# Gated linear attention and a gated MLP in one kernel: outputs issued in two steps, fewer dummy matmuls, a fused state update

## The chip, the cores and the metric

The kernel runs on one core of a Trainium2 chip. The engines that matter here are PE (matrix multiply, with weight loads as instructions of their own, PEld in the profile), DVE (elementwise vector work and scans), ACT (elementwise work with a lookup function), and SP, which here only issues transfers. PE writes to PSUM banks, DVE and ACT read them. The metric is the device time of one execution in microseconds, lower is better, as the median of several runs.

## What is computed

A recurrence over 768 tokens for 4 batches of 8 heads gives y; y, reordered to 3072 tokens of 256 features, goes through a gated MLP. The reference, cut to what matters:

```python
for c in range(nc):                      # chunks of 32 tokens
    cum = np.cumsum(log_a[chunk])
    M = (C @ B.T) * exp(cum_i - cum_j) * causal
    y = M @ x + (C @ state) * exp(cum)
    state = exp(sum(log_a)) * state + sum_j(B_j x_j * exp(cum_last - cum_j))
g = y @ w_gate                           # 3072 x 256 by 256 x 1536
out = (silu(g) * (y @ w_val)) @ w_out    # back to 256
```

x is 4 x 8 x 768 x 32, B and C have 16 states, all in float32.

## The kernel before

The tokens are cut into NB = 6 blocks of 128 (for each of the 4 batches), and the recurrence inside a block into K = 2 pieces of 64. For block k the attention part has these steps, by the names that tiles carry in the profile:

- L and E: running products of the decays, made by scans on DVE (`scan_j`, `scan_n`); for block 0 a part of the decays is spread over the partitions by PE first (`a`, `spread`). xb holds x and B, bc holds B and C; DVE weighs the B in xb by L (`weigh_b`) and the C in bc by E (`weigh_c`). Cz is C with the two heads of a pair apart.
- st: sums of B and x over a piece, on PE (`sums`); `apart` copies them into T, the state's tile, DVE one part and ACT the other.
- S: the scores C B on PE (`scores`); `mix` multiplies them into L, four DVE operations, called M in the plan.
- `step`: the state from one piece to the next, T = T + decay x older T.
- y: `outputs` puts, batch by batch, `values` (16 matmuls of L and xb) and `carried` (8 of bc and T) into four PSUM banks. In float32 each of these matmuls stands in the trace as two records, so a block's y are 192. For block 0 they are issued apart: first all `values` in two groups, then `carried`.

The MLP part then multiplies y with the weights:

- For block 0, y is copied as it is (xf), and used with the rounded float32 weights. For later blocks it is split into a high part xh and a low part xl in a shorter format, and each product is made of three matmuls (high x high, high x low, low x high).
- gv: gate and value matmuls, for NF = 12 groups f of 128 hidden columns, named gv k, f, and 0 or 1. In block 0 one matmul is two records. `silu` on ACT and `product` on DVE make sg. sg is split into hh (`hid_high`, ACT or DVE) and hl (`hid_low`, DVE).
- po: the output matmuls (`project`), `drain` copies them to ob, `store` sends them out.
- The weights arrive as 64-bit numbers. For each piece w DVE and ACT round them to float32 in about seven operations (`w_magnitude` to `w_round`); `w_high` (wh) and `w_low` (wl) split the result for blocks 1 to 5.

No instruction order is written out by hand. Every step is an entry of `plan.add`: engine, estimated cost, rank (a due time), what it needs, which buffers it takes and frees. `Plan.order` simulates the engines with these costs and issues on each engine, of the steps that could begin first, the one with the lowest rank; the list that comes out is each engine's program order, fixed when the program is built. `clocked` is its model of PE's speed: half speed until a window of 3.4133 us had been active enough (AWAKE). One engine name, "-", stands for steps without an instruction.

Dummies: `idle` issues three matmuls of a constant tile, unit, with itself (rest in the profile; nothing reads their result). The table IDLE gives their ranks in two lists: 23 entries (69 matmuls) before block 0's scores are mixed and 24 (72 matmuls) after.

Buffers: L, E, bc, xb and Cz exist once, so loads for a block wait for the outputs of the one before. T exists twice, tmp twice, PSUM banks are four for mm (gv, po, and S and y of block 0) and four for at (st, S and y, and the dummies). sg has SG = 21 places, and rounded weights w of the twelve gate groups take twelve of these until they are split.

Of the kernel before, what the change touches and what calls it, by code (L numbers as in the profile page):

```python
# [9 lines left out]
F32 = mybir.dt.float32  # L10
# [5 lines left out]
ALU = mybir.AluOpType  # L16
# [3 lines left out]
P = 128  # L20


Q = 64
K = P // Q
T = BATCH * P
# [17 lines left out]
class Plan:  # L43
# [5 lines left out]
    BIAS = 0.0  # L49
    WINDOW, AWAKE = 3.4133, 1.28  # L50
    SWITCH = {"Act": 1.28, "PE": 0.09}
# [51 lines left out]
    def clocked(self, t, cost, rows):  # L103

        while cost > 1e-9:
            w = int(t / self.WINDOW + 1e-9)
            rate = 1.0 if self.active.get(w - 1, 0.0) >= self.AWAKE else 0.5
            d = min(cost / rate, (w + 1) * self.WINDOW - t)
            self.active[w] = self.active.get(w, 0.0) + d * rate * rows
            cost -= d * rate  # L110
            t += d
        return t
# [90 lines left out]
def scan_moe_kernel(ctx: ExitStack, tc, aj, an, bc, xb, wgv, wo, cst, sel, out):  # L203
# [238 lines left out]
    def step(k, q):  # L442

        E = bl[k]["E"]
        t = att.tile([P, BATCH, 2 * D], F32, tag="tmp", name=f"tmp{k}_{q}", bufs=2)
        new = bl[k]["T"][:, q]
        decay = E[:, :, q, Q:].to_broadcast([P, BATCH, 2 * D])
        ve.tensor_tensor(out=t, in0=state(k, q), in1=decay, op=ALU.mult)
        ve.tensor_tensor(out=new, in0=new, in1=t, op=ALU.add)

# [31 lines left out]

    def outputs(k):
        for b in range(BATCH):
            values(k, (b,), (0, 1))
            carried(k, b)
# [179 lines left out]
    def do(f, *a):  # L666
        return lambda *e: f(*a, *e)


    plan = Plan(  # L670
        dict(mm=4, at=4, L=1, E=1, bc=1, xb=1, Cz=1, T=2, tmp=2, raw=4, w=1, x=2, hh=HB, sg=SG, ob=2),
        dict(SP=5.2, Act=3.0, DVE=1.0, PE=1.5, Pool=2.0, **{"-": 0.7}),
    )
# [30 lines left out]
    for i in range(NW):  # L704
# [8 lines left out]
        if i < NF:  # L713
            r = due(1, i) - LATER
        add([("Act", 0.6), ("DVE", 0.36)], None, do(w_high, i), r - 2.7, [("round", i)], gives=("wh", i))
        whole_done = [("gv", 0, i, m) for m in range(2)] if i < NF else []
# [8 lines left out]
    for k in range(NB):  # L725
# [20 lines left out]
        if not k:  # L746
# [4 lines left out]
            for b in range(BATCH):  # L751
# [6 lines left out]
                if b >= SPREAD:  # L758
                    add("DVE", 0.35, do(clip_j, b), r - 0.5, ["aj"], gives=("clip", b))
                    add("DVE", 1.14, do(scan_j, 0, b), r, [("clip", b), "dj"], gives=("L", 0, b))  # L760
            add("DVE", 0.35, clip_n, -1.4, ["an"], gives="clip_n")
            add("DVE", 1.17, do(scan_n, 0), -1.3, ["clip_n"], gives=("E", 0))
        else:
# [24 lines left out]
        for q in range(0 if k else 1, len(st)):  # L788
            need = [*before, ("E", k), ("ap", k, q)] + ([] if k or q > 1 else [("ap", k, 0)])
            add("DVE", 0.75, do(step, k, q), z + (8 if k else 25) + q, need, takes=[("tmp", ("tmp", k, q))], uses=[("tmp", k, q)] + ([("T", k - 1)] if k and not q else []), gives=("step", k, q))  # L790
            before = [("step", k, q)]
# [7 lines left out]
        if k:  # L799
            need = [*(("M", k, p) for p in range(NP)), ("ce", k), *steps]  # L800
            add("PE", 3.2, do(outputs, k), z + 11, need, takes=[("at", i) for i in y], uses=[L, *uses], gives=("y", k), kind="f", slack=SLACK)
        for b in range(0 if k else BATCH):
# [13 lines left out]
    for k in range(NB):  # L816
        xs = [(t, k, i) for t in ("xh", "xl") for i in range(2 * K)]
        for f in range(NF):
# [13 lines left out]
            h = ("h", k, f)  # L832
            add([("Act", 0.6), ("DVE", 0.36)], None, do(hid_high, k, f), r, [("pr", k, f)], takes=[("hh", h)], uses=[t], gives=("hh", k, f))
            add("DVE", 0.6, do(hid_low, k, f), r + 1, [("hh", k, f)], uses=[t, h], gives=("hl", k, f))
# [20 lines left out]
SPREAD = 3  # L855
IDLE = [-9.0] * 8 + [-3.8, -3.3, -2.8] + [-1.2 + 0.1 * i for i in range(12)], [15.0 + 0.5 * i for i in range(24)]
LATER = 3.0
# [55 lines left out]
```

## Time and profile before

| | us |
|---|---|
| median of 3 runs | 369.84 |
| lowest and highest run | 366.42, 373.3 |
| the profiled execution | 368.33 |
| its span, first to last instruction | 366.6 |
| PE busy | 357.5 (98%) |
| DVE busy | 231.0 (63%) |
| ACT busy | 127.0 (35%) |

The profile's busy time of PE contains dummies, and matmuls at half clock; it says when PE had something in it, not how much was done. The view of waits lists, for each engine and tile, what ended the idle time before it; "issue" means that nothing the profile shows did. The chain of waits is followed back from the last instruction and shown in order of time, neighbours merged. Every instruction carries line 192, the helper that records the order, so that work is told apart by tiles, not by lines.

### The profile page before, as it was taken

To read this page: it belongs to the slowest core of one execution; us is meant where nothing else is said; L and a number is where in the kernel's file an instruction comes from. 1 tells how busy PE (TensorE), PEld (TensorE's weight loads), DVE (VectorE), ACT (ScalarE), POOL (GpSimd) and SP (SyncE) were. 2 spreads that over 40 slices of the span, in tenths; PEclk is the share of its full clock that TensorE was granted. 3 is DMA by queue.
4 is the path that set the end of the run, shared out by engine and by line. 5 is a ranking of instruction groups with operands and counts; after the bars stand their busy time and mean duration, and the time that the engine had idled before them with its cause. 6 is when DMAs were issued, how large, how long until landed. Compare 5 with 4: busy or idle time off the path is not lost.

```text
span 366.6 us, 7587 instructions
## 1 busy us (share of the span) xinstructions
PE 357.5 (98%) x3293; PEld 276.0 (75%) x3293; DVE 231.0 (63%) x409; ACT 127.0 (35%) x225; POOL 0.8 (0%) x6
## 2 busy tenths in 40 slices
PE   8989999999999999999999999899999899999996
PEld 6855445488877888877788877688878688888895
DVE  3899999989999693663367554359345334352241
ACT  3275684444234543121342221323312133221242
POOL 0000000000000000000000000000000000000000
PEclk9999999999999999999999999899999999999999
DMA  6749742880101921000550000570100000100001
GB/s 181 283 134 285 240 146 87 237 224 2 58 2 46 207 95 59 0 3 2 172 119 25 35 2 2 143 148 2 57 0 3 4 0 2 57 0 2 0 0 59
DMA packets 8737, 28.62 MB, mean 78 GB/s; under 512 B 1008, under 2 KB 1912, under 8 KB 8064
## 3 DMA queue, kind: packets, MB, share of 16 engines
q1 hardware_dynamic: 8704, 28.14, 26.3%
q8 instruction: 26, 0.43, 0.5%
q14 instruction: 7, 0.06, 0.0%
HBM read 24.79 MB, written 3.35 MB: 77 GB/s over the span
## 4 chain that ended last, share of the span: by engine, by line
PE 94%; DVE 3%; issue 2%; ACT 0%; ACTq 0%
PE gv L192 55%; PE po L192 27%; PE y L192 5%; PE rest L192 3%; PE S L192 2%; PE a L192 1%; PE st L192 1%; DVE L L192 1%; DVE wo4w L192 0%; DVE sg L192 0%; DVE wo3w L192 0%; DVE wo4l L192 0%; DVE wo3l L192 0%; ACT wo5w L192 0%; ACT wo4w L192 0%
## 5 line engine op out<-in xcount | busy, mean ns | idle before, releaser
L192 DVE TENSOR_TENSOR sg<-gv,sg 128x512 f32<-128x512 f32 x72 | 49.4, 687 | 83.0 <-PE gv L192 80.6
L192 ACT ACTIVATE sg<-gv 128x512 f32<-128x512 f32 x72 | 42.9, 596 | 108.8 <-PE gv L192 108.6
L192 DVE TENSOR_TENSOR hl<-sg,hh 128x512 fp32r<-128x512 f32 x72 | 48.6, 685 | 17.5 <-ACT hh L192 17.0
L192 ACT CAST hh<-sg 128x512 fp32r<-128x512 f32 x56 | 34.9, 622 | 46.1 <-PE po L192 35.6
L192 DVE TENSOR_TENSOR_SCAN L<-L,dj 128x520 f32<-128x520 f32 x21 | 25.8, 1233 | 1.0 <-DMA L<-clipped 1.0
L192 DVE TENSOR_TENSOR L<-S,L 128x512 f32<-128x512 f32 x24 | 15.4, 682 | 2.2 <-PE S L192 2.2
L192 PEld LDWEIGHTS <-unit 128*128 128x128 bf16 x141 | 11.5, 122 | 4.9 <-issue 3.7
L192 PE MATMUL y<-L,xb 64*32 64x64 f32 x768 | 11.7, 223 | 3.2 <-issue 3.2
L192 ACT COPY ob<-po 128x512 f32<-128x512 f32 (+1 forms) x13 | 7.2, 555 | 21.3 <-PE po L192 20.8
L192 PE MATMUL rest<-unit 128*128 128x128 bf16 x141 | 12.9, 263 | 1.0 <-DVE warm L192 1.0
L192 PEld LDWEIGHTS y<-L,xb 64*32 64x32 f32 x768 | 7.6, 105 | 5.8 <-issue 3.9
L192 PE MATMUL y<-bc,T 32*64 32x64 f32 x352 | 10.2, 229 | 1.2 <-issue 1.2
L192 PEld LDWEIGHTS y<-bc,T 32*64 32x64 f32 x352 | 7.2, 131 | 4.5 <-issue 2.7
L192 PE MATMUL po<-hh,wo0h 128*128 128x512 f32 (+1 forms) x26 | 9.9, 382 | 0.0
L192 DVE CAST xh<-y 128x256 fp32r<-128x256 f32 x8 | 3.0, 418 | 10.9 <-PE y L192 10.9
L192 PE MATMUL po<-hh,wo2h 128*128 128x512 f32 (+1 forms) x26 | 9.8, 378 | 0.0
L192 PE MATMUL po<-hl,wo5h 128*128 128x512 f32 (+1 forms) x26 | 9.8, 377 | 0.0
L192 ACT CAST xh<-y 128x256 fp32r<-128x256 f32 x12 | 3.8, 379 | 17.1 <-PE y L192 17.1
L192 PE MATMUL po<-hl,wo0h 128*128 128x512 f32 (+1 forms) x26 | 9.7, 374 | 0.0
L192 PE MATMUL po<-hh,wo1h 128*128 128x512 f32 (+1 forms) x26 | 9.7, 373 | 0.0
L192 PE MATMUL po<-hl,wo3h 128*128 128x512 f32 (+1 forms) x26 | 9.7, 373 | 0.0
L192 PE MATMUL po<-hh,wo0l 128*128 128x512 f32 (+1 forms) x26 | 9.7, 373 | 0.0
(285 smaller groups left out, 800.5 us busy)
## 6 DMA issues: line engine op xcount, KB each, us to landing
L<-clipped SPq DMA_DIRECT2D x10, 520.0 KB
xb<-in_xb SPq DMA_DIRECT2D x6, 768.0 KB, 12.0
bc<-in_bc SPq DMA_DIRECT2D x6, 512.0 KB, 3.8
out<-ob SPq DMA_DIRECT2D x11, 256.0 KB, 2.2
E<-clipped SPq DMA_DIRECT2D x5, 260.0 KB
wg0r<-in_wgv SPq DMA_DIRECT2D x1, 512.0 KB
wg1r<-in_wgv SPq DMA_DIRECT2D x1, 512.0 KB
wg2r<-in_wgv SPq DMA_DIRECT2D x1, 512.0 KB, 9.9
```

Of the source, the lines that this page charges most:

```text
L192: ins = getattr(self.engine, name)(*a, **k)
```

## The change

- `outputs` takes the batches to do. For blocks 1 to 5 the plan has it twice, for batches 0 and 1 and for 2 and 3, with a step on an engine "~" of no instructions between them, which lets 2.6 us of planned time pass before the second half. The first half's slack against its inputs is larger.
- `step` is one fused multiply-add per batch, in place: four operations of 128 x 64 in place of two of 128 x 256. The buffer tmp goes.
- Splitting in block 0 is held back: `w_high` of the twelve gate weights and `hid_high` of block 0 need the last mix of block 1, ("M", 1, NP - 1).
- IDLE has 8 entries ahead and 14 with a rank of 1000, which are taken when PE has nothing else by the plan.
- The plan's clock is taken as slow before its time 17 (COLD). Ranks of `clip_n` and `scan_n` of block 0 are a little later, and the planned cost of `step` is 0.55 in place of 0.75.

```diff
-            rate = 1.0 if self.active.get(w - 1, 0.0) >= self.AWAKE else 0.5
+            rate = 1.0 if t >= self.COLD and self.active.get(w - 1, 0.0) >= self.AWAKE else 0.5
...
-        t = att.tile([P, BATCH, 2 * D], F32, tag="tmp", name=f"tmp{k}_{q}", bufs=2)
-        new = bl[k]["T"][:, q]
-        decay = E[:, :, q, Q:].to_broadcast([P, BATCH, 2 * D])
-        ve.tensor_tensor(out=t, in0=state(k, q), in1=decay, op=ALU.mult)
-        ve.tensor_tensor(out=new, in0=new, in1=t, op=ALU.add)
+        new, old = bl[k]["T"][:, q], state(k, q)
+        for b in range(BATCH):
+            ve.scalar_tensor_tensor(
+                new[:, b], old[:, b], E[:, b, q, Q:], new[:, b], ALU.mult, ALU.add
+            )
...
-    def outputs(k):
-        for b in range(BATCH):
+    def outputs(k, bs):
+        for b in bs:
             values(k, (b,), (0, 1))
             carried(k, b)
...
-        add([("Act", 0.6), ("DVE", 0.36)], None, do(w_high, i), r - 2.7, [("round", i)], gives=("wh", i))
+        later = [("M", 1, NP - 1)] if i < NF else []
+        add([("Act", 0.6), ("DVE", 0.36)], None, do(w_high, i), r - 2.7, [("round", i), *later], gives=("wh", i))
...
-            add("PE", 3.2, do(outputs, k), z + 11, need, takes=[("at", i) for i in y], uses=[L, *uses], gives=("y", k), kind="f", slack=SLACK)
+            add("PE", 1.6, do(outputs, k, (0, 1)), z + 11, need, takes=[("at", i) for i in y], uses=y, gives=("y", k, 0), kind="f", slack=min(k - 0.5, 2.5))
+            add("~", 2.6, lambda: None, z, [("y", k, 0)], gives=("pause", k))
+            add("PE", 1.6, do(outputs, k, (2, 3)), z + 11, [("pause", k)], uses=[L, *uses], gives=("y", k), kind="f")
...
-            add([("Act", 0.6), ("DVE", 0.36)], None, do(hid_high, k, f), r, [("pr", k, f)], takes=[("hh", h)], uses=[t], gives=("hh", k, f))
+            add([("Act", 0.6), ("DVE", 0.36)], None, do(hid_high, k, f), r, [("pr", k, f)] + ([] if k else [("M", 1, NP - 1)]), takes=[("hh", h)], uses=[t], gives=("hh", k, f))
...
-IDLE = [-9.0] * 8 + [-3.8, -3.3, -2.8] + [-1.2 + 0.1 * i for i in range(12)], [15.0 + 0.5 * i for i in range(24)]
+IDLE = [-9.0] * 8, [1000.0] * 14
```

What this does to the order is seen in the built programs. The dummies: before there are 141 of them (23 and 24 entries of three), in the change 66. Ahead of the first gv the change has the same 24 at the very start, then none until the outputs of block 0 are issued, and then 21; those that stood between the a matmuls (9), between st and y of block 0 (36) and within y (3) are gone, and st of block 0 stands whole ahead of its y, where half of it stood amid y. Between the gv of block 0 there were 45 up to the fourth group; the change has none up to the seventh, 9 behind it, and 12 ahead of S of block 1.

PE, around the outputs of block 3 (y3): before, the whole of y is followed by gv of group 9 of block 2.

```order
L192 MATMUL y3_2_1967<-bc3_1488,T3_1494 64x64
L192 MATMUL y3_3_1968<-bc3_1488,T3_1494 64x64
L192 MATMUL gv2_9_0_2066<-xh2_979,wg9h_887 128x512 x2
L192 MATMUL gv2_9_0_2066<-xh2_979,wg9l_966 128x512 x2
L192 MATMUL gv2_9_0_2066<-xl2_980,wg9h_887 128x512 x2
L192 MATMUL gv2_9_1_2086<-xh2_979,wg9h_887 128x512 x2
L192 MATMUL gv2_9_1_2086<-xh2_979,wg9l_966 128x512 x2
L192 MATMUL gv2_9_1_2086<-xl2_980,wg9h_887 128x512 x2
```

In the change the same gv stand behind batch 1, and the third batch's y follows.

```order
L192 MATMUL y3_2_1899<-bc3_1441,T3_1447 64x64
L192 MATMUL y3_3_1900<-bc3_1441,T3_1447 64x64
L192 MATMUL gv2_9_0_1950<-xh2_893,wg9h_839 128x512 x2
L192 MATMUL gv2_9_0_1950<-xh2_893,wg9l_884 128x512 x2
L192 MATMUL gv2_9_0_1950<-xl2_894,wg9h_839 128x512 x2
L192 MATMUL gv2_9_1_1957<-xh2_893,wg9h_839 128x512 x2
L192 MATMUL gv2_9_1_1957<-xh2_893,wg9l_884 128x512 x2
L192 MATMUL gv2_9_1_1957<-xl2_894,wg9h_839 128x512 x2
L192 MATMUL y3_0_1897<-L3_1445,xb3_1466 32x64
L192 MATMUL y3_2_1899<-L3_1445,xb3_1466 32x64
```

Blocks 4 and 5 are alike. In block 2 the twelve matmuls between the halves are po of block 0, in block 1 the four (eight records) of gv of block 0's group 10; y of block 1 begins behind group 9, where before it began behind group 8.

DVE, ahead of the first gv: before, this stands between the end of the mixing of block 0 and the copy of y (xf) that the first gv needs; ISA is the rounding addition.

```order
L192 TENSOR_TENSOR T0_108<-st0_1_220,cs_78 128x256
L192 TENSOR_SCALAR all_99<-all_99 128x6x64
L192 TENSOR_SCALAR wg0w_238<-wg0w_238 128x512
L192 TENSOR_SCALAR wg1w_306<-wg1w_306 128x512
L192 TENSOR_SCALAR wg0w_238<-wg0w_238 128x512
L192 TENSOR_SCALAR wg2w_375<-wg2w_375 128x512
L192 SCALAR_TENSOR_TENSOR wg0w_238<-wg0r_152,wg0w_238 128x512
L192 TENSOR_SCALAR wg2w_375<-wg2w_375 128x512
L192 ISA wg0w_238<-wg0r_152,wg0w_238 128x1024
L192 COPY xf_131<-y0_1_272 128x4x64
```

In the change (from wg1's first operation on) two more weight operations and a second copy come ahead of its end.

```order
L192 TENSOR_SCALAR wg1w_227<-wg1w_227 128x512
L192 TENSOR_SCALAR wg0w_195<-wg0w_195 128x512
L192 TENSOR_SCALAR wg2w_257<-wg2w_257 128x512
L192 SCALAR_TENSOR_TENSOR wg0w_195<-wg0r_145,wg0w_195 128x512
L192 TENSOR_SCALAR wg2w_257<-wg2w_257 128x512
L192 ISA wg0w_195<-wg0r_145,wg0w_195 128x1024
L192 SCALAR_TENSOR_TENSOR wg2w_257<-wg2r_153,wg2w_257 128x512
L192 TENSOR_SCALAR wg1w_227<-wg1w_227 128x512
L192 COPY xf_131<-y0_0_304 128x4x64
L192 COPY xf_131<-y0_1_305 128x4x64
```

Further ahead on DVE, the clip of L for the batch that is loaded directly moves from behind the third scan of block 0 to behind the first, and all four weighings of xb stand ahead of the scan of E and the mixes, where three stood between the mixes.

DVE, between the early gv of block 0: before, the splitting of groups 0 and 1 (wg0l, wg1l, hl) stands here, ahead of L of block 1.

```order
L192 TENSOR_TENSOR wg0l_513<-wg0w_238,wg0h_442 128x512
L192 ISA wg4w_470<-wg4r_429,wg4w_470 128x1024
L192 TENSOR_TENSOR sg0_1_504<-gv0_1_1_506,sg0_1_504 128x512
L192 TENSOR_TENSOR wg1l_544<-wg1w_306,wg1h_461 128x512
L192 TENSOR_TENSOR hl0_0_495<-sg0_0_456,hh0_0_494 128x512
L192 TENSOR_TENSOR hl0_1_547<-sg0_1_504,hh0_1_546 128x512
```

In the change it begins behind the last mix of block 1 (the first row), and hl of block 0 later still.

```order
L192 TENSOR_TENSOR L1_369<-S1_3_640,L1_369 128x4x2x64
L192 ISA wg10w_538<-wg10r_499,wg10w_538 128x1024
L192 TENSOR_SCALAR wg11w_594<-wg11w_594 128x512
L192 TENSOR_TENSOR wg0l_696<-wg0w_195,wg0h_689 128x512
L192 TENSOR_SCALAR wg11w_594<-wg11w_594 128x512
L192 TENSOR_TENSOR wg1l_753<-wg1w_227,wg1h_694 128x512
L192 SCALAR_TENSOR_TENSOR wg11w_594<-wg11r_540,wg11w_594 128x512
L192 TENSOR_TENSOR sg0_9_755<-gv0_9_1_684,sg0_9_755 128x512
L192 ISA wg11w_594<-wg11r_540,wg11w_594 128x1024
L192 TENSOR_TENSOR wg2l_769<-wg2w_257,wg2h_750 128x512
```

Of these twelve low halves ten stood behind the mixes before, too, from group 2 on. On SP the loads of block 2 change their order: bc goes ahead of L and E.

More of the change, by code (lines that the diff above doesn't have):

```diff
@@ L49 @@
     BIAS = 0.0
-    WINDOW, AWAKE = 3.4133, 1.28
+    WINDOW, AWAKE, COLD = 3.4133, 1.28, 17.0
     SWITCH = {"Act": 1.28, "PE": 0.09}
@@ L670, in scan_moe_kernel @@
     plan = Plan(
-        dict(mm=4, at=4, L=1, E=1, bc=1, xb=1, Cz=1, T=2, tmp=2, raw=4, w=1, x=2, hh=HB, sg=SG, ob=2),
-        dict(SP=5.2, Act=3.0, DVE=1.0, PE=1.5, Pool=2.0, **{"-": 0.7}),
+        dict(mm=4, at=4, L=1, E=1, bc=1, xb=1, Cz=1, T=2, raw=4, w=1, x=2, hh=HB, sg=SG, ob=2),
+        dict(SP=5.2, Act=3.0, DVE=1.0, PE=1.5, Pool=2.0, **{"-": 0.7, "~": 0.0}),
     )
@@ L760, in scan_moe_kernel @@
                     add("DVE", 1.14, do(scan_j, 0, b), r, [("clip", b), "dj"], gives=("L", 0, b))
-            add("DVE", 0.35, clip_n, -1.4, ["an"], gives="clip_n")
-            add("DVE", 1.17, do(scan_n, 0), -1.3, ["clip_n"], gives=("E", 0))
+            add("DVE", 0.35, clip_n, -1.15, ["an"], gives="clip_n")
+            add("DVE", 1.17, do(scan_n, 0), -1.12, ["clip_n"], gives=("E", 0))
         else:
@@ L789, in scan_moe_kernel @@
             need = [*before, ("E", k), ("ap", k, q)] + ([] if k or q > 1 else [("ap", k, 0)])
-            add("DVE", 0.75, do(step, k, q), z + (8 if k else 25) + q, need, takes=[("tmp", ("tmp", k, q))], uses=[("tmp", k, q)] + ([("T", k - 1)] if k and not q else []), gives=("step", k, q))
+            add("DVE", 0.55, do(step, k, q), z + (8 if k else 25) + q, need, uses=[] + ([("T", k - 1)] if k and not q else []), gives=("step", k, q))
             before = [("step", k, q)]
```

## The prediction

> **What bounds the kernel now.** I read the chain of waits first, its shares and then its pieces in time. It says that the end is set by the matmul engine.
>
> ```profile
> PE 94%; DVE 3%; issue 2%; ACT 0%; ACTq 0%
> ```
>
> PE is the bound, so what counts is time in which PE does nothing useful: waits, dummies, a lowered clock. The pieces show such time around the outputs (start, length, what, number of matmul records):
>
> ```profile
> 58.90 3.10 PE y L192 x192
> ...
> 227.11 2.58 PE y L192 x147
> 229.69 1.22 issue
> 230.92 0.83 PE y L192 x43
> 231.75 10.01 PE gv L192 x36
> ```
>
> The outputs y of block 1 are 192 small records in 3.10 us, at a stretch. The same 192 in block 4 take 2.58 + 1.22 + 0.83 = 4.63 us, with a hole put down to nothing ("issue"). The 36 records behind them take 10.01 us. The list of waits has the holes of all blocks:
>
> ```profile
> PE y L192 <- issue: 4.4, 4, 1.2
> ...
> DVE L L192 <- PE a L192: 2.8, 5, 1.2
> ...
> PEld S L192 <- DVE T L192: 0.3, 1, 0.3
> ```
>
> Four holes in y, 4.4 us. Which ones? I counted instructions between them (stretches from one hole to the next; the second and third column are PE's matmuls and weight loads with their counts), and took the instruction queue from the page's part 3:
>
> ```profile
> 20.50:174.20 153.70, 152.78 (x1527) 108.16 (x1527) 127.96 (x232) 65.70 (x119) 0.00 (x0) 1.00 0.37 108
> 174.20:230.30 56.10, 54.99 (x510) 44.19 (x509) 31.36 (x53) 15.84 (x28) 0.00 (x0) 1.00 0.21 58
> 230.30:288.00 57.70, 56.44 (x509) 45.54 (x509) 30.08 (x50) 15.97 (x28) 0.00 (x0) 0.97 0.23 56
> ```
>
> ```profile
> q8 instruction: 26, 0.43, 0.5%
> ```
>
> Between holes lie 3054, 1019 and 1018 instructions, the holes being in blocks 0, 3, 4 and 5. The page's 3293 matmuls and 3293 loads against 26 transfers on this queue make 253 per transfer, 16.5 KB each. So PE is fed in chunks of some 256 instructions, and the holes stand 12, 4 and 4 chunks apart (semaphore instructions, not counted here, fill the rest): all at the same place, a chunk's end. 192 y records are 384 instructions in 3.10 us, so a chunk made of y alone is used up in 256 / 384 x 3.10 = 2.07 us; with the 1.22 us hole, a new chunk comes about 3.3 us after the one before was begun. Counted on in steps of 256 from the hole of block 0, the chunks over y in blocks 1 and 2 also hold gv or po matmuls; there is no hole.
>
> What slows the records behind block 4's outputs is the clock. In the view by stretches the third number from the end is the share of the clock that is granted:
>
> ```profile
> 232.00:233.00 1.00, 1.00 (x4) 0.71 (x4) 1.00 (x4) 0.33 (x2) 0.00 (x0) 0.50 0.26 41
> ```
>
> **The change part by part.** *Outputs in two steps.* Twelve full-size gv or po records now stand between two halves of 96 y records (in block 1 eight gv records of block 0). Rows for the price:
>
> ```profile
> 144.05 16.32 PE gv L192 x72
> ...
> 161.15 1.60 PE gv L192 x6
> ```
>
> One record is 16.32 / 72 = 0.227 us, so twelve are 2.7 us. A chunk of 256 instructions at the halves now holds 192 of y (1.55 us) and the gv, 4.3 us or more, over the 3.3 a chunk needs. The holes go. In block 4 this saves 4.63 - 3.10 = 1.53 us, 0.31 more than the hole itself. The holes of blocks 3 and 5 are 4.4 less 1.22 and less at most 1.2 for block 0's: 2.0, and 0.25 to 0.3 more each: 2.5. Together -4.0 us. Block 0's hole is counted below. Against it: six gv between small matmuls take 1.60, not 1.36, so each such visit costs 0.24; five more visits, +1.2. Bounds: nothing, and 1.5. The drop of the clock goes with the hole: 36 records and a visit should take 36 x 0.227 + 0.24 = 8.4, so 10.01 - 8.4 = 1.6 us less; where the halves alternate with gv, no stretch without full-size matmuls is longer than 1.55 us. The first halves of x are not read sooner: x is cut when all of y is there, 2.7 us later, with 24 gv records and 16 us of po still ahead of its use.
>
> The Trainium skill, "Runtime: NRT & Kernel Launch", section "Instruction fetch mechanics", speaks against this: it says that refills of 256 instructions are hidden, and gives PE room for 2048. By it the split gains nothing and costs the visits. The block 4 rows above disagree with it.
>
> *Dummies.* Those between the gv of block 0 are run whether PE would wait or not:
>
> ```profile
> 22.83 3.49 PE gv L192 x8
> ...
> 35.92 13.79 PE gv L192 x32
> ```
>
> From 22.83 to 35.92 stand the gv of three column groups, 24 records of 13.79 / 32 = 0.431 = 10.3 us, in 13.1 us. Of the 2.8 us the change puts 21 dummies back later, between gv 6 and 9, 0.06 us each with two visits: 1.5. So -1.3. The cover is the weights being ready: the splittings and hl of groups 0 and 1 no longer stand ahead of weight rounding on DVE, so I see no wait in their place.
>
> *Start.* DVE's rows until the first gv, with those of the step:
>
> ```profile
> 4.99 0.70 DVE L192 TENSOR_TENSOR_SCAN L<-a,dj 128x260 f32<-128x260 f32 x1 [1.11 <-PE a L192]
> ...
> 7.34 0.40 DVE L192 TENSOR_SCALAR L<-L 128x512 f32<-128x512 f32 x1
> ...
> 15.01 0.68 DVE L192 TENSOR_TENSOR xb<-xb,L 128x128 f32<-128x128 f32 x3
> ...
> 18.44 0.42 DVE L192 TENSOR_TENSOR T<-st,cs 128x256 f32<-128x256 f32 x1 [1.22 <-PE st L192]
> ...
> 21.93 0.41 DVE L192 COPY xf<-y 128x256 f32<-128x256 f32 x1
> ...
> 25.00 0.41 DVE L192 TENSOR_TENSOR tmp<-T,E 128x256 f32<-128x256 f32 x1
> 25.45 0.42 DVE L192 TENSOR_TENSOR T<-T,tmp 128x256 f32<-128x256 f32 x1
> ```
>
> DVE loses two kinds of waits that dummies and order made: 2.8 - 1.1 = 1.7 on the a matmuls and 1.22 on st, which stood behind dummies and half of y. It gains a wait: the clip of L, which ran without one at 7.34, now stands right behind the scan that ends at 5.69, so at most 1.7 us. Ahead of the last xf now stand also a wg2 and a wg1 operation and one more copy; at 0.6, 0.35 and 0.35 (0.63 for 512 columns and two operands by a row below, the copy's 0.41 less its overlap) 1.3. Sum: -2.9 + 1.7 + 1.3 = +0.1 at the worst for the last xf, -1.6 if L is there in time; and PE, which came out of 24 dummies at 22.67 with xf there at 22.34, starts at once. I take -0.4 for the first gv (bounds -1.6 and +0.3). Block 0's hole of 1.22 lay beside this DVE work and gives nothing itself.
>
> *The fused step.* Two operations of 0.45 + 0.42 go, four of 128x64 come, for which no row exists: nearest is xb, 0.2 each at 128x128, so 0.4 to 0.8 against 0.87. I take 0.55: DVE gains 0.3 in ten steps, off the path: nothing, except before S of block 2, where PE waited 0.3 for T with DVE late; that goes, -0.3.
>
> *Loads.* SP issues block 2's L, E, bc and xb when y of block 1 is done and their places are free. Y of block 1 now ends two gv groups of block 0 later, about 5 us, and bc goes ahead of L. Behind L on DVE stand the products of block 1, which free the banks of PE.
>
> ```profile
> 78.15 1.24 DVE L192 TENSOR_TENSOR_SCAN L<-L,dj 128x520 f32<-128x520 f32 x1 [0.97 <-DMA L<-clipped]
> ```
>
> DVE already waited 0.97 here, with PE not held. SP was then also held by weight pieces that now come sooner, so I expect L about 2 us later, which the four banks just cover: 0, with 0 to 2 us as its bounds.
>
> *The clock of the first gv.* This is the part I know least.
>
> ```profile
> 13.22 3.88 PE L192 MATMUL rest<-unit 128*128 128x128 bf16 x36
> ...
> 21.32 1.51 PE L192 MATMUL rest<-unit 128*128 128x128 bf16 x24
> ```
>
> 36 dummies took 0.108 us each, 24 later ones 0.06: full speed came behind the 36, before the first gv. The change takes these 36 out and leaves 21 ahead of gv, about 2.2 us at the slow rate. If they are not enough, gv starts at half speed. The drop in block 4 was one stretch at about half speed, and cost 1.6 us. So 0 to 3.2 us (two stretches); nearest is one stretch, less for what the 21 dummies do: +1.2.
>
> The Trainium skill, "TensorE: Matmul & The Clock Gate", section on the HAM clock gate, lets the clock rise after one busy window of about 3.4 us whose phase is free; by it gv would be slow for up to such a window, at most 1.7 us. The 1.6 us of block 4 agrees.
>
> Sum: -4.0 + 1.2 - 1.6 - 1.3 - 0.4 - 0.3 + 1.2 = -5.2. The profiled execution took 368.33 (span 366.6 and 1.7 around it), which gives 363.1. That execution stands 1.5 below the median of 369.84; the runs, from 366.42 to 373.3, differ by about what one, two or more drops of the clock would make, and the new order has none. So 363.1 is forecast for the median: -1.8%.
>
> **Rivals.** *The clock is in time.* The 21 dummies and the y matmuls count enough. For it: full speed came before 21.32; against: the windows are fuller there before. Then 363.1 - 1.2 = 361.9, faster by 2.1%, and by more if the first gv comes earlier.
>
> *The holes stay*, because PE is held by something else there, or chunks come later than 3.3 us. For it: the profile names no releaser. Against: the three distances. Then 363.1 + 4.0, and 1.6 with the clock: 367 to 368.7, within 2%. The Trainium skill's "Runtime: NRT & Kernel Launch", cited above, would have it so.
>
> *Slower: the splitting held back comes too late.* The place is the end of block 0's gv. Behind block 1's last mix DVE has to do 13 operations of 512 columns on two operands and eight shorter ones (0.42, as T above) before the last xl, which the first gv of block 1 needs:
>
> ```profile
> 112.86 1.88 DVE L192 TENSOR_TENSOR hl<-sg,hh 128x512 fp32r<-128x512 f32 x3
> ```
>
> At 1.88 / 3 = 0.63 and 0.42 that is 11.5 us. PE has meanwhile the rest of gv 9 (3.5 less four mixes of 0.63: 1.0), two halves of y, and gv 10 and 11 with their visits: 1.0 + 3.1 + 7.0 + 0.5 = 11.6 us. It just holds, so each us more on DVE is lost to PE. For slower than 369.84 it takes 6.7 us more: the high halves, which ACT copies behind the last mix, and the low halves on DVE would have to follow each other instead of running side by side, so that sg's places and with them PE's banks come free one by one. A lateness of 1 to 3 us, here or by L of block 2, is more likely: 364 to 366.
>
> **How the numbers follow.** Forecast 0.5, clock in time 0.27, holes stay 0.08, splitting or L late 0.15 (0.02 of it slower than before by over 2%). About 2% is what a measurement of this kernel can tell from no change: below 362.4 is faster. That is the second case but for 0.02, and the lower part of the first (clock cost under 0.5), 0.15: 0.4. Slower 0.02, within 0.58. The range goes from 360.5 (clock in time, first gv 1.6 us earlier than before) to 365.9 (clock 3.2 and 0.8 of lateness), and leaves out the holes and a part of the late cases.
>
> **What would show it.** The chain's y pieces should be 96 records of 1.55 us with no "issue" between; a hole there refutes the chunks. The windows at blocks 3 to 5 should have a granted clock of 1.00. The first gv should start near 22.3; its eight records in 3.5 us mean the clock is in time, in 5 to 7 us that it is late. The first gv of block 1 should come with no wait on DVE xl or wl; one there means that the held-back splitting is late; a wait of DVE on L of block 2 over 2 us means the load is. If the time is below 360.5, PE lost more in the dummies or the holes than I counted.

## The result, and the profile after

The changed kernel takes 364.32 us (median of 14 runs, 361.59 to 366.12) where the kernel before takes 368.64 (14 runs, 365.73 to 373.3). The ratio is 0.9893, with a 95% interval of 0.9861 to 0.9925: 4.3 us or 1.1% less. That is clearly below 1, and under the 2% from which the prediction would have called it faster. The profiled execution took 363.95, with a span of 362.2; that of the kernel before 368.33 and 366.6. 363.1 was forecast.

The chain of waits of the changed kernel, by engine (shares of the span), no longer reads as PE alone:

```profile
PE 72%; DMA 14%; DVE 9%; SPq 2%; issue 2%; ACT 0%; DVEq 0%; ACTq 0%
```

PE had 94% of this line before. Where PE's share went can be read from the pieces of the chain in time, here around the outputs of block 4 and behind them, with the start of S of each later block as a mark (start us, length us, what):

```profile
106.25 1.17 PE S L192 x59
...
161.23 1.14 PE S L192 x63
...
216.93 1.14 PE S L192 x63
...
225.11 1.57 PE y L192 x94
226.68 2.95 PE gv L192 x12
229.63 1.50 PE y L192 x88
...
233.60 13.40 DMA xb<-in_xb
...
247.09 0.29 DVE xb L192
247.38 1.15 DVE L L192
248.53 0.59 DVE hl L192
...
249.17 5.51 PE po L192 x23
...
273.19 1.14 PE S L192 x63
```

Two things are to be seen. The outputs stand in two halves of 1.5 us with gv between, and there is no hole in them: what the change was forecast to do, it did. But behind them is a piece that the chain before did not have: the load of xb for the next block lands at 247.00, DVE weighs it, scans L, makes one hl, and only then can PE go on with po. The list of waits has this by engine and tile (total us, times, longest):

```profile
DVE xb L192 <- DMA xb<-in_xb: 5.4, 4, 2.2
...
DVE L L192 <- DMA L<-clipped: 3.4, 3, 1.6
...
PE po L192 <- DVE hl L192: 1.6, 2, 1.2
...
PEld gv L192 <- DVE sg L192: 1.1, 3, 0.7
...
PEld S L192 <- DVE T L192: 0.8, 1, 0.8
```

With the marks of the kernel before, from its chain,

```profile
108.01 1.17 PE S L192 x59
...
162.75 1.14 PE S L192 x63
...
218.94 1.14 PE S L192 x63
...
276.58 1.14 PE S L192 x63
```

the two executions can be cut into stages. The forecast column adds up the prediction's terms for each stage; the last column is the kernel e6_xb_late, an experiment below, whose marks are shown there.

| stage, us | before | after | gained | forecast | gained in e6 |
|---|---|---|---|---|---|
| start to first gv | 22.67 | 20.50 | 2.2 | 0.4 | 1.4 |
| first gv to S of block 2 | 85.34 | 85.75 | -0.4 | 0.2 | 1.3 |
| S of block 2 to S of block 3 | 54.74 | 54.98 | -0.2 | -0.2 | -0.2 |
| S of block 3 to S of block 4 | 56.19 | 55.70 | 0.5 | 1.0 | 1.2 |
| S of block 4 to S of block 5 | 57.64 | 56.26 | 1.4 | 2.9 | 2.9 |
| S of block 5 to the end | 90.02 | 89.01 | 1.0 | 1.0 | 1.1 |
| sum | 366.6 | 362.2 | 4.4 | 5.2 | 7.8 |

The first gv of the changed kernel, in PE's timeline (start, length, what, number of records, idle time before it), begins 2.2 us earlier than before, and its second group of eight is already at the rate of all later ones:

```profile
20.50 4.07 PE L192 MATMUL gv<-xf,wg0w 128*128 128x512 f32 x8
24.40 3.60 PE L192 MATMUL gv<-xf,wg1w 128*128 128x512 f32 x8
27.84 2.74 PE L192 MATMUL gv<-xf,wg2w 128*128 128x512 f32 x6
```

From one group to the next it is 3.90, then 3.44 us. The lengths that a timeline shows overlap; the differences of the starts are the rate. Why the first group took longer is told further down.

### The profile page after: what moved, and what is told of

Read it like the earlier page. It is cut to its first block, busy times and chain, and to the rows that moved or that the text cites. A ratio compares the mean times of both kernels' runs of the same rounds, so it can differ in the third digit from the quotient of the medians.

```text
span 362.2 us, 7458 instructions
## 1 busy us (share of the span) xinstructions
PE 352.9 (97%) x3218; PEld 269.7 (74%) x3218; DVE 232.0 (64%) x429; ACT 127.4 (35%) x225; POOL 0.8 (0%) x6
## 4 chain that ended last, share of the span: by engine, by line
PE 72%; DMA 14%; DVE 9%; SPq 2%; issue 2%; ACT 0%; DVEq 0%; ACTq 0%
PE gv L192 44%; PE po L192 21%; DMA xb<-in_xb 11%; PE y L192 4%; DVE L L192 2%; SPq L192 2%; DMA wg1r<-in_wgv 2%; PE S L192 2%; DMA bc<-in_bc 1%; DMA wo5r<-in_wo 1%; PE st L192 1%; DVE wo3w L192 1%; DVE sg L192 1%; DVE wo1w L192 1%; DVE xb L192 0%
## 5 line engine op out<-in xcount | busy, mean ns | idle before, releaser
L192 ACT CAST hh<-sg 128x512 fp32r<-128x512 f32 x54 | 33.7, 624 | 39.6 <-PE po L192 29.3
L192 ACT ACTIVATE Cz<-bc,cs 128x512 f32<-128x512 f32 x12 | 8.0, 718 | 10.7 <-DMA bc<-in_bc 10.7
L192 PE MATMUL po<-hl,wo4h 128*128 128x512 f32 (+1 forms) x26 | 9.9, 382 | 1.6 <-DVE hl L192 1.6
L192 DVE TENSOR_TENSOR xb<-xb,L 128x128 f32<-128x128 f32 x24 | 6.6, 286 | 5.4 <-DMA xb<-in_xb 5.4
L192 PE MATMUL po<-hh,wo3h 128*128 128x512 f32 (+1 forms) x26 | 9.8, 377 | 0.0
L192 PE MATMUL po<-hh,wo4h 128*128 128x512 f32 (+1 forms) x26 | 9.7, 374 | 0.0
L192 PE MATMUL po<-hl,wo1h 128*128 128x512 f32 (+1 forms) x26 | 9.7, 374 | 0.0
L192 PE MATMUL po<-hl,wo2h 128*128 128x512 f32 (+1 forms) x26 | 9.7, 373 | 0.0
L192 PE MATMUL po<-hh,wo4l 128*128 128x512 f32 (+1 forms) x26 | 9.7, 373 | 0.0
```

The costliest lines, as they stand in the source:

```text
L192: ins = getattr(self.engine, name)(*a, **k)
```

## The experiments

The theory I began with: the gain is in the holes, which are PE running out of instructions at the end of a chunk of 256, and part of it is taken back by a wait that the split makes. DVE works in order, xb's weighing stands ahead of some hl, and the load of xb is now issued some 3 us later, when the second half of y is done. The first rival is that the holes belong to something that certain blocks do; the second, that the loss belongs to another part of the change, or was there before. The first half of the theory stood; of the second half the wait stood and its cause did not. Ratios are always to the kernel before, run on the same chip.

### One part of the change at a time

*Outputs in two steps alone* (e1), in the kernel before:

```diff
-            add("PE", 3.2, do(outputs, k), z + 11, need, takes=[("at", i) for i in y], uses=[L, *uses], gives=("y", k), kind="f", slack=SLACK)
+            add("PE", 1.6, do(outputs, k, (0, 1)), z + 11, need, takes=[("at", i) for i in y], uses=y, gives=("y", k, 0), kind="f", slack=min(k - 0.5, 2.5))
+            add("~", 2.6, lambda: None, z, [("y", k, 0)], gives=("pause", k))
+            add("PE", 1.6, do(outputs, k, (2, 3)), z + 11, [("pause", k)], uses=[L, *uses], gives=("y", k), kind="f")
```

> The kernel before with the outputs in two steps and nothing else. Theory (fetch): the three holes of 1.2 us in y of blocks 3, 4 and 5 go, the one in block 0 stays, and granted clock stays at 1.00 in block 4; that is -3.7 for holes and slowed rows and -1.6 for the clock, +1.2 for five more visits: -4.1 us. Of that the new wait seen in the changed kernel (loads of the next block issued about 3 us later, DVE waiting on xb ahead of hl, PE's po waiting on hl) takes back 1.5 to 3 if it belongs to the split: ratio 0.993 to 0.997, with PE po waiting on DVE hl in blocks 3 and 4. Rival 1: that wait belongs to the lead that fewer dummies give: ratio 0.989 and no such wait. Rival 2 (the holes are not a matter of the instructions' count): holes stay, ratio 1.003.

Measured: ratio 0.9947 (0.9913 to 0.998), median 366.28. No hole in blocks 1 to 5, and the wait is there, this time in blocks 2 and 3. Its chain:

```profile
123.59 12.89 DMA xb<-in_xb
...
143.13 2.81 PE po L192 x11
...
181.73 12.78 DMA xb<-in_xb
...
194.60 0.29 DVE xb L192
...
196.69 5.53 PE po L192 x23
```

So the wait needs no other part of the change. But it is not in the same blocks.

*Fewer dummies alone* (e2), with the planner's cold clock and the two ranks:

```diff
-IDLE = [-9.0] * 8 + [-3.8, -3.3, -2.8] + [-1.2 + 0.1 * i for i in range(12)], [15.0 + 0.5 * i for i in range(24)]
+IDLE = [-9.0] * 8, [1000.0] * 14
```

> The kernel before with the changed dummies (and the planner's cold clock and the two ranks that go with them), outputs whole. Theory (fetch in chunks of 256 instructions): 148 instructions fewer ahead of block 1 shift the chunk ends, so the holes move: about 1.2 us each in y of blocks 1 and 2, at most 0.2 in block 3, none in blocks 4 and 5, where the kernel before had them. Time: dummies -1.3 and first gv -1.7 to -2.2, holes -1 or so, the clock +-1.6: ratio 0.987 to 0.994. Rival (the holes belong to something that blocks 3 to 5 do): they stay in y of blocks 3, 4 and 5, ratio 0.991 to 0.992.

Measured: ratio 0.9932 (0.9896 to 0.9967), median 365.35. The outputs were left whole, and the holes moved, as the theory of chunks said. In its chain, block 2 has one and blocks 3 and 4 (and 5, not shown) run through:

```profile
112.99 2.60 PE y L192 x160
115.59 0.81 issue
...
171.42 3.08 PE y L192 x187
...
227.54 3.12 PE y L192 x190
```

PE's timeline has the hole of block 1, which is not on the part of the chain that is shown:

```profile
63.56 0.42 PE L192 MATMUL y<-L,xb 64*32 64x64 f32 x21 [1.17 <-issue]
```

This kernel has the wait on xb too, in block 3, though its outputs are whole. Its chain:

```profile
177.33 12.74 DMA xb<-in_xb
190.17 0.29 DVE xb L192
...
192.25 8.44 PE po L192 x35
```

That speaks against the split as the cause.

*Holding back alone* (e3):

```diff
-        add([("Act", 0.6), ("DVE", 0.36)], None, do(w_high, i), r - 2.7, [("round", i)], gives=("wh", i))
+        later = [("M", 1, NP - 1)] if i < NF else []
+        add([("Act", 0.6), ("DVE", 0.36)], None, do(w_high, i), r - 2.7, [("round", i), *later], gives=("wh", i))
```

> The kernel before with block 0's and the weights' splitting held back until block 1's last mix, nothing else. Theory (off the path): PE's instruction count is the same up to 2, so the four holes stay in y of blocks 0, 3, 4 and 5; time within 0.3 us, ratio 0.999 to 1.001. Rival 1: holding back delays the first gv of block 1: ratio over 1.003 with PE gv waiting on DVE. Rival 2: it frees DVE for the rounding, gv of block 0 runs closer: ratio 0.996 or less.

Measured: ratio 0.997 (0.9932 to 1.0008), median 367.09; holes in blocks 0, 3, 4 and 5 as before. Within the interval it is worth nothing; up to 0.7% is not excluded.

*The fused step alone* (e4):

```diff
-        ve.tensor_tensor(out=t, in0=state(k, q), in1=decay, op=ALU.mult)
-        ve.tensor_tensor(out=new, in0=new, in1=t, op=ALU.add)
+        for b in range(BATCH):
+            ve.scalar_tensor_tensor(new[:, b], old[:, b], E[:, b, q, Q:], new[:, b], ALU.mult, ALU.add)
```

> The kernel before with the fused state step alone. Theory: four 128x64 operations take as long as the pair they replace (0.88 against 0.87 in the changed kernel's block 0), all off the path but for the 0.3 us that PE waited for T: ratio 0.999 to 1.000. Rival: the step frees DVE by 0.3 us in each of ten places and this reaches PE: ratio 0.996 or less.

Measured: ratio 1.0004 (0.9958 to 1.0051). It moves the time by nothing that shows; 0.4% either way is not excluded.

### Moving the chunks and nothing else

Twelve more entries (e5) at the head of the dummies' table put 36 matmuls and their 36 loads where PE waits for data anyway:

```diff
-IDLE = [-9.0] * 8 + [-3.8, -3.3, -2.8] + [-1.2 + 0.1 * i for i in range(12)], [15.0 + 0.5 * i for i in range(24)]
+IDLE = [-9.0] * 20 + [-3.8, -3.3, -2.8] + [-1.2 + 0.1 * i for i in range(12)], [15.0 + 0.5 * i for i in range(24)]
```

> The kernel before with twelve more dummies (72 instructions on PE) at its very start, nothing else; they lie in the time in which PE waits for block 0's data. Theory (fetch in chunks of 256 instructions, 3.25 us from one to the next): chunk ends move by 72 instructions, so the holes of about 1.2 us move from y of blocks 3, 4 and 5 to y of blocks 1, 2 and 3; y of blocks 4 and 5 run through in 3.1 us. Rival (something those blocks do): holes stay in blocks 3, 4 and 5. Time: same sum of holes, so 368 to 371.

Measured: 369.84 in one execution, where the kernel before has 368.55 on this chip. In its chain, block 2 has a hole that the kernel before has not, and blocks 3, 4 and 5, which have them before, run through:

```profile
116.27 2.91 PE y L192 x177
119.17 1.10 issue
...
175.54 3.08 PE y L192 x182
...
231.64 3.08 PE y L192 x182
...
287.48 3.12 PE y L192 x190
```

Block 1 has one of 0.76 in PE's timeline, behind its 180th record. The rival falls: the same instructions in the same blocks have a hole or none by how many instructions ran ahead of them. One thing was forecast wrongly: block 3 should have had one, since a chunk of y alone ends behind its 139th record there. That chunk began only 11 records into y; why it was there in time is open.

Counted in the programs as built (matmuls, weight loads and semaphore instructions of PE), every hole over 0.7 us in the outputs of any of the profiled kernels stands where the count is 192 or 193 more than a multiple of 256: 3 in the blocks behind block 0 in the kernel before, 2 with fewer dummies, 2 with the shift, and so on. No kernel with the outputs in two steps has one in blocks 1 to 5.

### Taking the wait away

One number in the planner (e6): DVE's weighing of xb counts on its load 6 us later, from block 2 on, and so is put behind hl.

```diff
-            add("DVE", 0.21, do(weigh_b, k, b), z + 1.0 + b if k else -1.2, [("L", k, b), ("xb", k)], gives=("bt", k, b))
+            add("DVE", 0.21, do(weigh_b, k, b), z + 1.0 + b if k else -1.2, [("L", k, b), ("xb", k)], gives=("bt", k, b), slack=6.0 if k > 1 else 0.0)
```

> The changed kernel with one number in the planner: from block 2 on, DVE's weighing of xb counts on the load 6 us later, so it stands behind all of hl and not between hl and hl. Nothing else moves. Theory (the new wait): DVE waiting for xb in the order ahead of hl is what PE's po wait for in blocks 3 and 4 (2.5 us in the profiled run); with xb behind hl that wait is gone, and no one needs xb for 20 us: 1.5 to 2.5 us off the changed kernel, ratio to before 0.982 to 0.986, PE po with no wait on DVE hl in blocks 2 to 4. Rival (the wait only covers another one, such as hh's four places or PE's own order): ratio stays 0.989.

Measured: ratio 0.9797 (0.9751 to 0.9844), median 360.85, and six runs between 360.18 and 361.14. It beats both kernels, and its interval lies below that of the changed kernel. In its chain, PE runs from the second half of block 1's y on without a stop to the last po:

```profile
66.53 36.31 PE gv L192 x152
...
105.23 1.14 PE S L192 x63
...
160.15 1.14 PE S L192 x63
...
180.06 16.32 PE po L192 x72
...
215.09 1.14 PE S L192 x63
...
235.04 16.32 PE po L192 x72
...
269.86 1.14 PE S L192 x63
```

The 72 po records of blocks 2 and 3 take 16.32 each, the bare rate. Its list of waits has, for all that DVE waits on xb, and nothing of PE po on DVE hl:

```profile
DVE xb L192 <- DMA xb<-in_xb: 0.3, 1, 0.3
```

The gain, 3.5 us between the medians and 3.4 between the spans, is more than the 1.5 to 2.5 that was expected. In the profiled execution of the changed kernel the wait also stood in the gv of block 1, where DVE waited for L and xb of block 2 ahead of the products sg that free PE's banks: from the end of block 1's y to S of block 2 this kernel takes 105.23 - 66.53 = 38.7 us, the changed kernel 106.25 - 66.01 = 40.2. In that stretch PE's weight loads wait three times for DVE in the changed kernel (0.29, 0.67 and 0.77 us), and not at all here.

*Is the wait worth the same in the kernel before?* The same edit there (e9), with 10 us in place of 6, since its loads are planned earlier:

> The kernel before with DVE's weighing of xb behind hl (10 us later in the planner here, since its loads are planned earlier), nothing else. Theory 1 (the wait was already in the kernel before, in some runs, and spreads its times from 366 to 373): the spread shrinks to about 1 us and the ratio is 0.992 to 0.997. Theory 2 (the wait came with the change alone): ratio 0.999 to 1.001 and the same spread.

Measured: ratio 1.0012 (0.998 to 1.0045), runs from 365.92 to 370.9. That is theory 2's number: in the kernel before the wait costs 0.7 us at the most by the interval, and it is not what spreads that kernel's runs. But theory 2's mechanism, that the wait came with the change, does not stand beside the chain of e2. So the two were put side by side, block by block: when DVE begins with xb, counted from the end of y, and how late PE is at the po behind it. PE is due there 16.8 us after the end of y in both kernels. Before, 36 gv records follow y, 8.4 us, and xb stands ahead of hl 6, which the 38th record of po reads: 37 records before it, 37 x 0.227 = 8.4. In the changed kernel 24 gv follow, 5.7 us, but the planner puts xb ahead of hl 8, which the 50th record reads: 49 x 0.227 = 11.1. DVE's work from xb to the end of hl is 2.1 us (0.29, 1.15, 0.59 and a little between), so xb may come 14.7 us after y and no later.

| kernel, block | xb after the end of y, us | late by the rule | PE came late by |
|---|---|---|---|
| before, 3 | 189.70 - 175.31 = 14.4 | 0 | 0.2 |
| before, 4 | 246.64 - 231.75 = 14.9 | 0.2 | 0 (36 gv took 10.0, not 8.4) |
| fewer dummies alone, 3 | 190.17 - 174.50 = 15.7 | 1.0 | 1.0 |
| split alone, 3 | 194.60 - 178.89 = 15.7 | 1.0 | 1.0 |
| holding back alone, 4 | 248.51 - 232.97 = 15.5 | 0.8 | 0.8 |
| changed, 3 | 190.61 - 175.47 = 15.1 | 0.4 | 0.4 |
| changed, 4 | 247.09 - 231.13 = 16.0 | 1.3 | 1.3 |

The rule holds in every row within 0.2 us. It also holds in three kernels that the table leaves out: e5 (blocks 3 and 4: xb after 15.6 us, PE late by 0.9 and 0.8), e7 (block 3: 16.1 and 1.4) and e8 (block 3: 15.5 and 0.8), and where xb came within 14.7 us in blocks 3 and 4 PE lost 0.3 us at the most. e5 is the kernel before with its chunks moved, so the wait can cost that kernel 1.7 us in one execution. DVE's wait in the kernel before, in its timeline, is the first of these:

```profile
189.70 0.29 DVE L192 TENSOR_TENSOR xb<-xb,L 128x128 f32<-128x128 f32 x1 [1.53 <-DMA xb<-in_xb]
```

So the cover is as thin before as after, and the same loads land 13.5 to 16.1 us after y in all these kernels. In the kernel before a part of it is hidden behind records slowed by the clock: the 36 gv of block 4 took 10.01 in place of 8.4, and PE came to po later than the load. With the holes and the drops away, nothing hides it. Between kernels with and without the edit the gain is 0.0054 for the split alone, 0.0046 for the dummies alone, 0.0030 and 0.0096 for the changed kernel without and with holding back: 1.1 to 3.5 us, each uncertain by about 2. That it is as little as 0 to 0.7 in the kernel before, though e2, e3 and e5 show single waits of about a microsecond, would follow if the clock drops cover the rest; this is argued, not shown.

*Outputs in two steps, with xb behind hl* (e10; the planner's number is 6 us here), against the run just told:

> The kernel before with xb behind hl and the outputs in two steps. Theory (with the wait gone the split shows its own worth, -4.1 us by the prediction's terms): 4.1 us or 0.011 below the kernel before with xb behind hl alone, where the split alone gained 0.005. Rival (the split is worth only the holes, 3.4, less the visits, 1.2): 2.2 us or 0.006 below it.

Measured: 0.9893 (0.9851 to 0.9935), median 363.21. That is 0.0119 or 4.4 us below 1.0012, the theory's 0.011; the rival's 0.006 lies at the edge of what the two intervals allow. The split alone, with the wait, had gained 0.005.

*Fewer dummies, with xb behind hl* (e11):

> The kernel before with xb behind hl and the changed dummies. Theory: dummies 1.3 and the earlier start 1.7 to 2.2, and holes 2.4 in place of 3.4: 3.5 to 4.5 us or 0.010 to 0.012 below the kernel before with xb behind hl alone. Rival (the start's lead is lost in block 0's gv and on the loads of block 2): 1.3 to 2.3 us or 0.004 to 0.006 below it.

Measured: 0.9886 (0.9847 to 0.9925), median 363.39. That is 0.0126 or 4.6 us below 1.0012, just above the upper end of what the theory said. The first gv starts at 21.75 (23.48 in e9), and the holes are two in place of four.

### Undoing one part of the change

*Outputs in one step again* (e7), all else as changed:

> The changed kernel with the outputs in one step again. Theory (fetch): holes of 1.2 us in y of blocks 1 and 2 (there, not where the kernel before has them) and at most 0.2 in block 3: +2.5 us, less 1.2 for visits saved, and loads issued 3 us earlier, which takes 0 to 2.5 of the wait on xb away: ratio 0.987 to 0.993. Rival (holes gone for another reason, such as dummies or the held-back splitting): no hole in any y but block 0's, ratio 0.985 or less.

Measured: 0.9906 (0.9855 to 0.9958), median 364.96. The holes come back, in blocks 1 and 2 as the count said, though not in those in which the kernel before has them:

```profile
59.87 2.58 PE y L192 x155
62.45 0.99 issue
...
111.85 2.60 PE y L192 x160
114.45 0.80 issue
```

The time is that of the changed kernel within the intervals. With the new dummies there are two holes left for the split to remove, 0.99 + 0.80 = 1.8 us, and it costs five visits of 0.2: what the split is worth hangs on where the chunks end.

*Without holding back* (e8), as changed, and (e12) with xb behind hl:

> The changed kernel without the holding back of the first block's splitting. Theory (holding back is off the path): ratio 0.989 as the changed kernel, gv of block 0 at 3.43 us a group. Rival 1 (holding back gives DVE the time that the weights' rounding needs now that dummies are gone): PE gv of block 0 wait on DVE wg or sg, ratio 0.992 or more. Rival 2 (holding back makes products and loads of block 2 late, as the 1.3 us lost in gv of block 1 suggest): ratio 0.986 or less.

> The changed kernel with xb behind hl and without the holding back of the first block's splitting. Theory (holding back is off the path): ratio 0.980, within 0.002 of the same with it (0.9797). Rival 1 (holding back gains): 0.984 or more. Rival 2 (it costs, by the 1.3 us lost in gv of block 1): 0.976 or less.

Measured: 0.9884 (0.9823 to 0.9945), where the changed kernel has 0.9893; and 0.9854 (0.9813 to 0.9895), where the same with holding back has 0.9797 on another chip. The two profiled executions with xb behind hl have spans of 358.9 without and 358.8 with holding back, and the same lengths of all stages within 0.3 us. So the first run says that holding back is worth nothing. The second, by its ratio, is the first rival's number, 2 us lost without it, but the intervals overlap and the stages show no place for such a loss. Whether it helps by a part of a per cent stays open.

## Why the prediction was right, and where it was not

The sum came out 1.2 us above the forecast, 364.32 against 363.1, inside the range. It came out so by luck, because errors went against each other: the gains were larger than forecast by some 2.6 us (7.8 in e6 against 5.2), 2.1 of it ahead of S of block 2, and one cost that was priced at nothing was about 3.5. The mechanism of the holes was right; three steps failed: what the first gv waits for, its clock, and the loads.

**The holes.** Right. They are at chunks' ends: they moved when instructions were added or taken out far ahead of them, and they went when full-size matmuls were put between. The changed kernel's stages and those of e6 give the sizes: blocks 3, 4 and 5 gain 1.2, 2.9 and 1.1 us once the new wait is away, where 1.0, 2.9 and 1.0 were forecast. The Trainium skill, "Runtime: NRT & Kernel Launch", section "Instruction fetch mechanics", has these refills hidden; that holds here while a chunk of 256 lasts longer than about 3.3 us, and not for a chunk of small matmuls that is used up in 2.1. The 3.3 is not the whole rule: the holes in y of blocks 1 to 5 measured 0.76 to 1.49 us, the one of block 4 1.22 in the kernel before and 0.85 in e9 with the same count ahead of it, and one expected hole, in block 3 of e5, did not come. The rival that the holes stay is out.

**The visits.** 0.24 was forecast for each; S of block 2 to S of block 3, where nothing but a visit was added, takes 54.92 in e6 and 54.74 before: 0.2.

**The clock in block 4.** Right: the granted clock stays at 1.0 there, and 24 gv records take 5.66 in e6, the full rate. The slowed records are not fixed to block 4 of the kernel before, either: in e9 the 36 records behind the hole of block 4 took 8.39, and in e4 it is block 5 whose 36 took 9.84. So the 1.6 us were read from one place in one execution; that about as much is gained on the average can be seen from the runs. Of the runs of the kernel before that enter the ratios, the 17 with a mean granted clock of 0.998 or more have a median of 366.97, the 20 with 0.993 to 0.995, as in the profiled execution, 368.85. None of the 14 runs of the changed kernel is in the second group.

**Dummies.** The 21 in place of the 45 between the gv stand at 45.16 and 53.69 as counted, and take 0.50 and 0.67 us of the chain, where the 45 took 2.8; gv 1 to 6 take 3.44 us each. The first three groups of the kernel before took 13.1, these 10.8.

**The first gv.** This step failed in what it took PE to wait for. Forecast was 0.4 us earlier, with bounds of 1.6 and -0.3. In the profiled execution it is 2.2 earlier, in the other kernels with the new dummies the first gv starts at 21.2 to 22.6, with the old ones at 22.7 to 23.5. DVE's work was sized about right: the waits on the a matmuls fell to 1.2 us, the wait on st went, and the clip of L waited for its load as foreseen, 1.25 us. The last two copies of xf, in DVE's timeline of the changed kernel, are

```profile
20.91 0.76 DVE L192 COPY xf<-y 128x256 f32<-128x256 f32 x2
```

and end at 21.67, where the last of before ended at 22.34: 0.7 earlier, near the 0.4. But the first gv no longer needs the last xf. In the programs as built its first matmul (two records) reads one half of xf; before, ACT and DVE each copied a part of that half, in the change ACT copies all of it, and DVE's two copies make the half that the second matmul reads. So the first gv starts at 20.50, and PE waits for DVE only ahead of the second matmul:

```profile
PEld gv L192 <- DVE xf L192: 1.0, 1, 1.0
```

The second group then begins at 24.40, where in the kernel before the first eight records end at 22.67 + 3.49 = 26.16.

**The clock of the first gv.** This step failed too: 1.2 us were priced in for half speed, and there was none. The first group took 3.90 in place of 3.44, but the 0.5 is the wait for xf. The granted clock, third from the end, is 1.00 in the stretch of that wait:

```profile
21.00:22.00 1.00, 0.85 (x3) 0.28 (x2) 1.00 (x4) 0.00 (x0) 0.00 (x0) 1.00 0.69 201
```

In e2, e11 and e12 the first group took 3.54, in e6 3.57; e6 has a granted clock of 0.50 up to 21 us and 0.99 in the microsecond behind it, in which its first gv starts. The 36 dummies that were taken out do not make sure of the clock: with them, in e9, it is 0.50 from 23 to 25 us, behind a hole of 1.90 in y of block 0, and the first eight gv took 4.58 in the chain, where the kernel before shows 3.49. By the rule cited from "TensorE: Matmul & The Clock Gate" in the Trainium skill the loss would be anything up to 1.7; the 0 here and the 1.1 of e9 both lie within that. The rival of the clock in time was right, and the sign that the prediction named for it, eight records in 3.5 us, was hidden by the wait for xf.

**The fused step.** The step's price was wrong, and it did not matter. 0.55 us was taken for four operations of 128x64; in DVE's timeline of the changed kernel they take

```profile
23.37 0.88 DVE L192 SCALAR_TENSOR_TENSOR T<-T,E 128x64 f32<-128x64 f32 x4
```

0.88 or, to the start of what follows, 0.79, as long as the pair they replace (0.87). Alone the step moves the time by nothing (1.0004). The 0.3 us that PE waited for T did not go: that wait is 0.8 now, and belongs to the loads, since e6 has none.

**Loads.** This is the step that failed most: "0, with 0 to 2 us as its bounds". It looked at block 2 alone, counted on PE's banks to cover it, and asked what the change moves. In block 2 it was too small: the 40.2 us against 38.7 above make 1.5, inside the bounds, and the sign that was named for it, a wait of DVE on L of over 2 us, did not show (1.33). The later blocks were not looked at, because the wait of DVE on xb there cost PE almost nothing in the one execution shown. But PE's cover was 14.7 us and the load took 14.4 and 14.9; in block 4 the slowed clock behind the hole covered the rest. In the changed kernel the load took 15.1 and 16.0 and PE lost 0.4 and 1.3. Nothing shows that the change made the load later: in blocks 3 and 4 it took 13.7 to 15.6 in the kernel before, e3, e4 and e5, and 13.5 to 16.1 in the kernels with the split or the new dummies. Taking the wait away gave 3.5 us in the changed kernel (3.4 between the profiled spans; by the ratios uncertain by about 2, and 1.1 without holding back), so this one term came near the whole gain that was measured. The rival "splitting or L late, 364 to 366" had the right time and the right kind of cause, a load behind which DVE stands; about half of the cost was in the place that it named, block 2, the other half behind blocks 3 and 4.

**Holding back.** No wait of PE in its place, as forecast, and no gain that is shown.

## What to carry to other kernels

When a change takes stalls away from the engine that bounds a kernel, the next wait behind it is already in the profile: an engine that works in order and stands waiting for a transfer costs nothing only while the bound is later than it. Work out for each such wait how much cover is left, and whether the stall to be removed was part of it; then order the waiting step behind what others need. Holes of about a microsecond with no releaser, in stretches of many small instructions, are worth counting in instructions: if they come at a fixed count, a few instructions more or fewer anywhere ahead move them, and longer instructions put among them remove them.

## What was not expected of the hardware

- Whether a hole appears depends on where in a chunk of 256 instructions a stretch of y begins: 72 instructions more at the start moved two of them from blocks 4 and 5 to blocks 1 and 2, and took that of block 3 away.
- Four fused operations of 128x64 on DVE take as long (0.88 us) as two plain ones of 128x256 (0.87): half the elements passed through in the same time.
- The same loads for the next block (bc, L, E and xb) were in 14.4 us after the end of y in one block and 16.0 in another, with the same 584 packets, 2.64 MB, on that queue in the stretch of each; against a cover of 14.7 us that difference decides whether PE waits in a block.
